# Layer 1 of a linear-attention block: sums of the last rows led ahead, denominators and scalings of two chunks placed among the other sums

## The chip, the cores and the metric

The kernel runs on one core of one Trainium2 chip. The metric is the device time in microseconds. TensorE (PE) multiplies matrices into PSUM; VectorE (DVE) and ScalarE (ACT) empty PSUM and work element by element; GpSimdE (POOL) does some of the normalisation; SyncE (SP) issues the transfers. Each engine takes its own instructions in order, and engines wait for each other with semaphores.

## The reference

Four layers run one after another on x of 2048 rows and 576 columns: linear attention (A), a two-layer perceptron with GELU (B), and A and B again with the same weights. Each is added to its input and takes a layernorm of it (B a second one). The change is in the first A alone:

```python
qkv = x @ wqkv                                # 32 heads of 18 columns
phi = lambda t: jnp.where(t > 0, t + 1, jnp.exp(t)) + 1e-6
pq, pk = phi(q), phi(k)
kv = jnp.einsum("bhsd,bhse->bhde", pk, v)
z = jnp.einsum("bhsd->bhd", pk)
num = jnp.einsum("bhqd,bhde->bhqe", pq, kv)
den = jnp.einsum("bhqd,bhd->bhq", pq, z)[..., None] + 1e-6
o = num / den                                 # then @ wo
```

## The kernel before

Rows go in 16 tiles of 128 (`NT`), queries in 4 chunks of 512 (`NCA`), and the 576 columns of heads in 5 groups: four of 7 heads (126 columns) and one of 4 (72 columns). v is never formed. The kernel sums y^T phi(k) over all rows, where y is the normalised input, and multiplies by the weights of v afterwards.

- `q_proj(g, c)` (L611) makes the queries of group g and chunk c, with five 512-column products into one PSUM bank (`q_ps`), and phi of them: two ScalarE passes (L547, L548), then VectorE's minimum and maximum (L553, L555), which writes `pq`.
- `rows_by_keys(t, half)` (L659) adds row tile t to the sums for one half (288) of the key columns. Chunks 0 to 3 are four 128-column blocks of y, in two pairs of PSUM banks; chunk 4, "the tail", is the last 64 columns of y and a column of ones, whose row of the sums is z. The sums leave PSUM behind the last tile: L681 for the tail, L684 for the others.
- `kv_groups` (L686) multiplies the sums by the weights of v and keeps the blocks of a head (`kvT`); `kv_wo_half` (L709) and `kv_wo` (L796) multiply this by wo (`kvwo`), in halves of 288 columns. The first uses single banks, the second pairs of banks.
- The z stage (L787 to L794) spreads z over the heads into `zsel`. `den_stage(c)` (L812) makes the denominators of chunk c with twenty small products and their reciprocals with ScalarE (logarithm L824, exponential L827), into the one tile `rden`. `quad_stage` (L832) spreads these on VectorE.
- `scale_stage(g, c)` (L842) spreads reciprocals over the rows of group g with one 512-column product, ScalarE copies them (L851), VectorE multiplies `pq` (L852). `quarter_stage(c)` (L856) does so for groups 0 to 3 at once: sixteen small products (32 rows of the array) into four single banks, and four ScalarE copies into the buffer `turned` (L867); `quarter_scale` (L869) multiplies (L873).
- `wo_stage(t)` (L878) makes row tile t of the output with ten 288-column products (L883), and VectorE adds the residual (L598).

PSUM has two pools: `ps_h`, four single banks with the tag "h", used in turn by `q_ps`, `k_ps`, the tail, `z_ps`, `den_ps`, `kv_ps`, `kvwo_half`, `rden_ps` and transposes; and `ps_acc`, two pairs, "accA" and "accB". A new tile waits until the last reader of the tile that had its bank is through.

The order on TensorE is the order of the program here: `pe(...)` chains its instructions. In layer 1, `q_left` holds the 20 pairs (g, c); 16 are done when the pass of the second half begins. This pass adds all 16 row tiles with their tails, with `kv_groups((0, 1))` behind tile 6 and four `kv_wo_half` behind tiles 8 to 11. After it come z, a projection, the denominators of chunk 0, `kv_groups((2, 3, 4))`, a projection, `kv_wo` and the spreads of chunk 0 in turn, a projection, the denominators of chunk 1, the last projection, and the `wo_stage` of tiles 0 to 15. Chunk 1 is spread behind tile 1 and scaled behind tile 2 (`quarter_stage(1)`, `quarter_scale`), chunks 2 and 3 later in the same way. The first tiles of the next layer's normalised rows are transposed among the last `wo_stage`s (L493), behind a chain over VectorE or ScalarE (statistics), GpSimdE (L428 to L469) and back.

Of the kernel before, what the change touches and what calls it, by code (L numbers as in the profile page):

```python
# [8 lines left out]
ALU = mybir.AluOpType  # L9
# [6 lines left out]
P = 128  # L16
NT = S // P
# [17 lines left out]
def build(tc, A_x, A_wqkv, A_wo, B_w1, B_b1, B_w2, B_b2, out, dbg=None, n_layers=4):  # L35
    nc = tc.nc
    dbg = dbg or {}
    with ExitStack() as ctx:
# [569 lines left out]
        def layer_A(li, next_kind, pre_a1=None):  # L608
            pq = {}

            def q_proj(g, c, defer=False):  # L611
                qp = ps_h.tile([P, 512], F32, name="q_ps", tag="h")
                for k in range(KD):
                    pe(nc.tensor.matmul(qp[0:GR[g], :], lhsT=wqkv_sb[:, k, GO[g]:GO[g] + GR[g]],  # L614
                                     rhs=yT[:, k, c * CA:(c + 1) * CA],
                                     start=(k == 0), stop=(k == KD - 1)))
                pq[(g, c)] = first_pq if first_pq is not None and (g, c) == (0, 0) else \
                        blk.tile([P, D], BF16, name="pq", tag="blk")
                if g == 0:
                    if first_pq is None or c > 0:  # L620
                        (nc.gpsimd if li > 0 else nc.vector).memset(pq[(g, c)][96:P, 0:CA], 1.0)
                phi = lambda after=None, dve_after=None, exp_first=False: phi_from_psum(qp[0:GR[g], :], pq[(g, c)][0:GR[g], 0:CA], GR[g], CA,
                                                       turned_cols=(li > 0), after=after, dve_after=dve_after,
                                                       exp_first=exp_first)
                if defer:
                    return phi
                phi()
# [31 lines left out]
            def rows_by_keys(t, half, chunks=(4, 0, 1, 2, 3)):  # L659
# [10 lines left out]
                if 4 not in chunks:  # L670
                    return
# [8 lines left out]
                cols = slice(half * HALF, (half + 1) * HALF)  # L680
                nc.scalar.copy(out=k2[4][0:65, cols], in_=self_k["tail"][0:65, 0:HALF])  # L681
# [27 lines left out]
            def kv_wo_half(g, half):  # L709
# [5 lines left out]
                copy = nc.vector.tensor_copy if half else nc.scalar.copy  # L715
                copy(out=kvwo[g][0:GR[g], half * HALF:(half + 1) * HALF], in_=wp[0:GR[g], 0:HALF])

            if li == 0:
                def keys(t):
                    k_half(t, 0)  # L720
                    k_half(t, 1)

                def feed_and_tick(t, n):
                    feed0(t, after=dve_last["phi"] if t > 5 else None)
                    for _ in range(n):
                        lnp.tick()

                k_half(0, 0)
                lnp.tick()
                phi = k_half(0, 1, defer=True)  # L730
                k_half(1, 0)
                feed_and_tick(3, 2)
                k_half(1, 1)
                phi()
                rows_by_keys(0, 0, (0, 1, 2, 3))
                keys(2)
                feed_and_tick(4, 2)
                rows_by_keys(1, 0, (0, 1, 2, 3))
                rows_by_keys(2, 0, (0, 1, 2, 3))
                k_half(3, 1)  # L740
                k_half(3, 0)
                q_proj(*q_left.pop(0))
                phi = q_proj(*q_left.pop(0), defer=True)
                feed_and_tick(5, 1)
                feed_and_tick(6, 2)
                phi(after=first_ones["ca4"].ins.name)
                in_order("s0a s0b g0 s1a s1b n0 nt0 g1 cd0 n1 nt1 s2a s2b g2 cd1 mi00 s3a n2 nt2 s3b ma00 g3 u3 mi10 s4a "
                         "mi11 n3 ma11 nt3 mi20 ma10 ma20 mi21 s4b ma21 g4 u4 mi01 ma01 s5a s5b mi30 g5 mi31 u5 ma30 ma31")
                in_order("ln0 re0 ln1 re1 ca0 e00 ca1 ln2 re2 id00 e01 e10 ca2 e11 id10 e20 e21 ca3 e31 e30 id30 ca4")
                rows_by_keys(3, 0, (0, 1, 2, 3))  # L750
                for t in range(4):
                    rows_by_keys(t, 0, (4,))
                for t in range(4, NT):
                    keys(t)
                    pre_a1(t)
                    if t == 4:
                        lnp.tick()
                    masks(2)
                    q_proj(*q_left.pop(0), defer=True)(after=act_last["turned"])
                    lnp.tick(transposes=0)  # L760
                    rows_by_keys(t, 0)
                for _ in range(2):
                    q_proj(*q_left.pop(0))
                masks(len(mask_steps))
            LAG = 3
            steps = [(t, 1) for t in range(NT)] if li == 0 else [(t, half) for half in range(2) for t in range(NT)]
            behind = []
            for n, (t, half) in enumerate(steps):
                if li == 0:
                    if t in (0, 1, 2):  # L770
                        wide_masks(t)
                    rows_by_keys(t, 1)
                else:
                    pre_a1(t)
                    k_half(t, half)
                    behind.append((t, half))
                    if n % 2 == 1:
                        q_proj(*q_left.pop(0))
                    if len(behind) > LAG:
                        rows_by_keys(*behind.pop(0))  # L780
                if half and t == 6:
                    kv_groups((0, 1))
                if half and t in (8, 9, 10, 11):
                    kv_wo_half((t - 8) // 2, t % 2)
            while behind:
                rows_by_keys(*behind.pop(0))
            zp = ps_h.tile([P, 512], F32, name="z_ps", tag="h")  # L787
            for g in range(G):
                pe(nc.tensor.matmul(zp[0:GR[g], g:g + 1], lhsT=k2[4][:, GO[g]:GO[g] + GR[g]], rhs=ident[:, 64:65],
                                    start=True, stop=True))  # L790
            nc.vector.tensor_tensor(out=zsel[0:126, 0:4, :], in0=head_sel[0:126, 0:4, :],
                                    in1=zp[0:126, 0:4].unsqueeze(2).to_broadcast([126, 4, H]), op=ALU.mult)
            nc.vector.tensor_tensor(out=zsel[0:72, 4, :], in0=head_sel[0:72, 4, :],
                                    in1=zp[0:72, 4:5].to_broadcast([72, H]), op=ALU.mult)  # L794

            def kv_wo(g):  # L796
                wp = ps_acc.tile([P, 2, 512], F32, name="kvwo_ps", tag=("accB", "accA")[g % 2])
                for half in range(2):
                    pe(nc.tensor.matmul(wp[0:GR[g], half, 0:HALF], lhsT=kvT[0:GR[g], g, 0:GR[g]],
                                     rhs=wo_sb[0:GR[g], g, half * HALF:(half + 1) * HALF], start=True, stop=True))  # L800
                kvwo[g] = blk.tile([P, D], BF16, name="kvwo", tag="blk")
                out = kvwo[g][0:GR[g], :].rearrange("p (h n) -> p h n", h=2)
                if g in (3, 4):
                    nc.vector.tensor_copy(out=out, in_=wp[0:GR[g], :, 0:HALF])
                else:
                    act_last["kvwo"] = nc.scalar.copy(out=out, in_=wp[0:GR[g], :, 0:HALF]).ins.name
# [70 lines left out]

            def wo_stage(t):  # L878
# [16 lines left out]
            phi = q_proj(*q_left.pop(0), defer=True)  # L895
# [273 lines left out]
```

## Time and profile before

| | us |
|---|---|
| three runs | 762.37, 762.40, 762.41 |
| the profiled execution, its own time | 762.86 |
| its span, first to last instruction | 761.1 |
| TensorE busy | 755.4 |
| ScalarE busy | 327.4 |
| VectorE busy | 271.2 |
| pass of the second half, first to last start | 58.87 to 69.63 |
| first `wo_ps` / first product of the next layer | 78.18 / 102.98 |

Times within the profile count from the start of the span. A row of the timeline gives the start, the length, the engine, the line, the operation, out<-in with partitions and elements, the number of instructions merged into it, and in brackets the idle time of that engine before it and what ended it. Matmuls overlap each other in time, so the cost of one is the distance from its start to the next start. The granted clock of TensorE is 1.00 throughout.

### The profile page before, as it was taken

How to read it: one execution, taken by the hardware profiler on the slowest of the kernel's cores; microseconds unless marked ns; L12 is line 12 of the kernel's file. 1: busy time of each engine (PE TensorE's matmuls, PEld its weight loads, DVE VectorE, ACT ScalarE, POOL GpSimd, SP SyncE). 2: the span in 40 equal slices, each digit the busy share in tenths (PEclk: the TensorE clock that was granted, in tenths of full speed). 3: DMA queues.
4: the chain of work that ended last, by engine and by line, in shares of the span. 5: the costliest groups of instructions: out<-in, count | busy, mean ns of one | idle time of the engine just before them, and what ended most of it. 6: DMA issues, size and time to landing. Idle time of an engine off the chain costs nothing.

```text
span 761.1 us, 15693 instructions
## 1 busy us (share of the span) xinstructions
PE 755.4 (99%) x6539; PEld 489.0 (64%) x6539; DVE 271.2 (36%) x683; ACT 327.4 (43%) x731; POOL 119.1 (16%) x194
## 2 busy tenths in 40 slices
PE   8999999999999999999999999999999999999998
PEld 5777654774477457646777767447645754674476
DVE  8875962136023503401455678600230132000000
ACT  6884756205600650263056566560164036205600
POOL 4840341002000301200100005300020020001000
PEclk9999999999999999999999999999999999999999
DMA  8992573017302711320246007530240033011000
GB/s 255 267 309 51 169 269 83 16 58 196 82 31 84 185 53 47 108 69 16 73 122 202 1 32 244 193 83 16 76 104 29 16 125 83 9 32 55 2 10 23
DMA packets 80897, 73.82 MB, mean 97 GB/s; under 512 B 36730, under 2 KB 65466, under 8 KB 80826
## 3 DMA queue, kind: packets, MB, share of 16 engines
q1 hardware_dynamic: 80826, 72.82, 32.9%
q8 instruction: 51, 0.84, 0.5%
q14 instruction: 20, 0.16, 0.1%
HBM read 48.03 MB, written 24.77 MB: 96 GB/s over the span
## 4 chain that ended last, share of the span: by engine, by line
PE 94%; DMA 2%; DVE 2%; ACT 1%; issue 0%; SPq 0%; DVEq 0%; ACTq 0%
PE m_ps L1060 36%; PE h_ps L1002 20%; PE hp_ps L1002 16%; PE q_ps L614 6%; PE k_ps L644 5%; PE k_ps L669 4%; PE wo_ps L883 2%; PE m_half L1060 1%; PE k_tail L669 1%; DMA xo<-x_d 1%; DMA x_d<-xo 1%; PE tp L493 1%; ACT turned L867 1%; DMA x<-in_A_x_dram 0%; PE kv_ps L693 0%
## 5 line engine op out<-in xcount | busy, mean ns | idle before, releaser
L1060 PE MATMUL m_ps<-w_sb,hT 128*128 128x288 bf16 x2232 | 274.8, 286 | 0.0
L1060 PEld LDWEIGHTS <-hT 128*128 128x128 bf16 x2304 | 224.8, 98 | 59.8 <-issue 3.4
L1002 PEld LDWEIGHTS <-w_sb 64*128 64x128 bf16 x2304 | 124.5, 94 | 136.5 <-issue 1.9
L1002 PE MATMUL hp_ps<-yT,w_sb 64*128 64x512 bf16 x1152 | 178.0, 376 | 0.0
L1002 PE MATMUL h_ps<-yT,w_sb 64*128 64x512 bf16 x1152 | 148.0, 376 | 0.0
L1007 ACT COPY relay_sb<-relay_sb 128x1 f32<-128x1 f32 x144 | 28.6, 198 | 260.2 <-PE h_ps L1002 217.9
L998 ACT ACTIVATE hT<-h_ps,b1T 128x512 bf16<-128x512 f32 x144 | 91.2, 684 | 44.4 <-PE h_ps L1002 44.4
L428 POOL TENSOR_TENSOR ln_rstd<-ln_u,neg_half 128x1 f32<-128x1 f32 x61 | 35.4, 581 | 408.3 <-DVE ln_u L410 225.3
L998 ACT ACTIVATE hT<-hp_ps,b1T 128x512 bf16<-128x512 f32 x144 | 91.2, 693 | 0.0
L598 DVE TENSOR_TENSOR xbf<-m_ps,xo 128x576 bf16<-128x576 f32 x15 | 11.4, 758 | 212.9 <-PE m_ps L1060 212.9
L598 DVE TENSOR_TENSOR xo<-m_ps,xo 128x576 f32<-128x576 f32 x16 | 12.1, 757 | 176.5 <-PE m_ps L1060 176.5
L581 POOL TENSOR_TENSOR xo<-xo,b_bc 128x576 f32<-128x576 f32 x32 | 40.9, 1284 | 101.3 <-DMA xo<-x_d 62.7
L1002 PE MATMUL h_ps<-yT,w_tail 64*128 64x512 bf16 x144 | 54.1, 376 | 0.0
L1002 PE MATMUL hp_ps<-yT,w_tail 64*128 64x512 bf16 x144 | 54.1, 376 | 0.0
L614 PE MATMUL q_ps<-yT,wqkv_sb 128*126 128x512 bf16 (+1 forms) x200 | 49.5, 379 | 0.0
L644 PE MATMUL k_ps<-wqkv_sb,yT 128*128 128x288 bf16 x320 | 47.0, 286 | 0.3 <-ACT yT L495 0.3
L883 PE MATMUL wo_ps<-kvwo,pq 126*128 126x288 bf16 (+1 forms) x320 | 44.5, 286 | 0.2
L1002 PEld LDWEIGHTS <-w_tail 64*128 64x128 bf16 x288 | 27.1, 94 | 17.1
L644 PEld LDWEIGHTS <-yT 128*128 128x128 bf16 x320 | 30.9, 98 | 8.9 <-ACT yT L495 1.0
L883 PEld LDWEIGHTS <-pq 126*128 126x128 bf16 (+1 forms) x320 | 29.8, 97 | 10.3 <-DVE pq L873 0.7
L614 PEld LDWEIGHTS <-wqkv_sb 128*126 128x126 bf16 (+1 forms) x200 | 25.4, 131 | 11.8
L295 DVE STREAM_TRANSPOSE turned<-y_ring 128x576 bf16<-128x576 bf16 x40 | 30.3, 766 | 0.4
(141 smaller groups left out, 595.7 us busy)
## 6 DMA issues: line engine op xcount, KB each, us to landing
xo<-x_d SPq DMA_DIRECT2D x48, 288.0 KB
x_d<-xo SPq DMA_DIRECT2D x32, 288.0 KB
xl<-x_d SPq DMA_DIRECT2D x24, 288.0 KB
y_d<-turned SPq DMA_DIRECT2D x40, 144.0 KB
w_sb<-in_B_w_dram SPq DMA_DIRECT2D x6, 864.0 KB
yT<-y_d SPq DMA_DIRECT2D x10, 512.0 KB
w_sb<-in_B_w_dram SPq DMA_DIRECT2D x9, 512.0 KB
x_d<-xn SPq DMA_DIRECT2D x16, 288.0 KB
```

The costliest lines, as they stand in the source:

```text
L295: turn = nc.vector.transpose(out=turned[:, :, j, :], in_=y[:, 0:D])
L428: nc.gpsimd.tensor_tensor(out=rstd[:], in0=it["u"][:], in1=neg_half[:], op=ALU.pow)
L581: nc.gpsimd.tensor_tensor(out=xo[:], in0=xo[:], in1=b2_bc[:], op=ALU.add)
L598: total = nc.vector.tensor_tensor(out=xn[:, cols].rearrange("p (h n) -> p h n", h=2), in0=halves, in1=xo[:, cols].rearrange("p (h n) -> p ...
L614: pe(nc.tensor.matmul(qp[0:GR[g], :], lhsT=wqkv_sb[:, k, GO[g]:GO[g] + GR[g]], rhs=yT[:, k, c * CA:(c + 1) * CA], start=(k == 0), stop=(k ...
L644: pe(nc.tensor.matmul(kp[:, 0:HALF], lhsT=yT[:, k, t * P:(t + 1) * P], rhs=wqkv_sb[:, k, D + half * HALF: D + (half + 1) * HALF], start=(k ...
L669: pe(nc.tensor.matmul(dst, lhsT=lhsT, rhs=pk, start=(t == 0), stop=(t == NT - 1)))
L883: pe(nc.tensor.matmul(wp[:, half, 0:HALF], lhsT=pq[(g, c)][0:GR[g], j * P:(j + 1) * P], rhs=kvwo[g][0:GR[g], half * HALF:(half + 1) * HALF ...
L998: act_last["gelu"] = nc.scalar.activation(out=to, in_=ps, func=ACT.Gelu_apprx_tanh, bias=b1T[:, f:f + 1], scale=1.0).ins.name
L1002: mm = pe(nc.tensor.matmul(dst[n], lhsT=wt, rhs=mv, start=(seen[n] == 0), stop=(seen[n] == 8)))
L1007: relay = nc.scalar.copy(out=relay_sb[:, 1:2], in_=relay_sb[:, 0:1])
L1060: pe(nc.tensor.matmul(acc[half][:, 0:HALF], lhsT=hT[f][:, j * P:(j + 1) * P], rhs=w2_sb[:, f, half * HALF:(half + 1) * HALF], start=(f == ...
```

## The change

In layer 1 alone, the pass of the second half is reordered. All sixteen tails come first, and their sums are copied out as soon as they are complete. The four-block sums follow, tile by tile, and among them are placed: z, the denominators of chunks 0 and 1, their quarter stages, the spread of group 4, all scalings of the two chunks, `kv_groups((0, 1))`, four `kv_wo_half` and two of the last four projections. Groups 0 to 3 of chunk 0 are spread by a quarter stage, where there were four `scale_stage`s. Behind the pass stay a projection, `kv_groups((2, 3, 4))`, the last projection and six `kv_wo_half` on single banks, where `kv_wo` used pairs of banks. The buffer of `pq` is now taken when phi is run and not when the products are. The second attention layer keeps its order.

```diff
@@ -614,14 +614,15 @@
...
-                pq[(g, c)] = first_pq if first_pq is not None and (g, c) == (0, 0) else \
+
+                def phi(after=None, dve_after=None):
+                    pq[(g, c)] = first_pq if first_pq is not None and (g, c) == (0, 0) else \
...
-                phi = lambda after=None, dve_after=None, exp_first=False: phi_from_psum(qp[0:GR[g], :], pq[(g, c)][0:GR[g], 0:CA], GR[g], CA,
...
+                    phi_from_psum(qp[0:GR[g], :], pq[(g, c)][0:GR[g], 0:CA], GR[g], CA, turned_cols=(li > 0), after=after,
+                                  dve_after=dve_after)
+
                 if defer:
                     return phi
                 phi()
...
-            def rows_by_keys(t, half, chunks=(4, 0, 1, 2, 3)):
+            def rows_by_keys(t, half, chunks=(4, 0, 1, 2, 3), done=True):
 
...
                     dst = self_k["tail"][0:65, 0:HALF] if k == 4 else self_k["acc"][k // 2][:, k % 2, 0:HALF]
                     lhsT = (tail_of(t) if li > 0 else first_tail(t)) if k == 4 else row_of[t][:, k * P:(k + 1) * P]
                     pe(nc.tensor.matmul(dst, lhsT=lhsT, rhs=pk, start=(t == 0), stop=(t == NT - 1)))
-                if 4 not in chunks:
+                cols = slice(half * HALF, (half + 1) * HALF)
+                if 4 in chunks and t == NT - 1:
+                    nc.scalar.copy(out=k2[4][0:65, cols], in_=self_k["tail"][0:65, 0:HALF])
+                if not done:
                     return
                 if t % 2:
                     del self_k["pk"][(half, t // 2)]
@@ -677,8 +681,6 @@
                         x0_tiles.clear()
                 if t < NT - 1:
                     return
-                cols = slice(half * HALF, (half + 1) * HALF)
-                nc.scalar.copy(out=k2[4][0:65, cols], in_=self_k["tail"][0:65, 0:HALF])
                 for i, copy in enumerate((nc.scalar.copy, nc.vector.tensor_copy)):
                     for j in range(2):
                         copy(out=k2[2 * i + j][:, cols], in_=self_k["acc"][i][:, j, 0:HALF])
...
-            def kv_wo_half(g, half):
+            def kv_wo_half(g, half, by_dve=None):
                 wp = ps_h.tile([P, 512], F32, name="kvwo_half", tag="h")
...
-                copy = nc.vector.tensor_copy if half else nc.scalar.copy
-                copy(out=kvwo[g][0:GR[g], half * HALF:(half + 1) * HALF], in_=wp[0:GR[g], 0:HALF])
...
-            LAG = 3
-            steps = [(t, 1) for t in range(NT)] if li == 0 else [(t, half) for half in range(2) for t in range(NT)]
-            behind = []
-            for n, (t, half) in enumerate(steps):
-                if li == 0:
-                    if t in (0, 1, 2):
-                        wide_masks(t)
-                    rows_by_keys(t, 1)
...
-                if half and t == 6:
-                    kv_groups((0, 1))
-                if half and t in (8, 9, 10, 11):
-                    kv_wo_half((t - 8) // 2, t % 2)
-            while behind:
-                rows_by_keys(*behind.pop(0))
-            zp = ps_h.tile([P, 512], F32, name="z_ps", tag="h")
...
+                by_dve = half if by_dve is None else by_dve
+                copy = nc.vector.tensor_copy if by_dve else nc.scalar.copy
+                copy = copy(out=kvwo[g][0:GR[g], half * HALF:(half + 1) * HALF], in_=wp[0:GR[g], 0:HALF])
+                if not by_dve:
+                    act_last["kvwo"] = copy.ins.name
+
+            def z_stage():
+                zp = ps_h.tile([P, 512], F32, name="z_ps", tag="h")
+                for g in range(G):
+                    pe(nc.tensor.matmul(zp[0:GR[g], g:g + 1], lhsT=k2[4][:, GO[g]:GO[g] + GR[g]], rhs=ident[:, 64:65],
+                                        start=True, stop=True))
...
+            if li == 0:
+
+
+                for i in range(3):
+                    wide_masks(i)
+                for t in range(NT):
+                    rows_by_keys(t, 1, (4,), done=False)
+                left = list(range(NT))
+
+                def sums(n):
+                    for _ in range(n):
+                        rows_by_keys(left.pop(0), 1, (0, 1, 2, 3))
+
+                sums(2)
+                z_stage()
+                sums(2)
+                den_stage(0)
+                quad_stage(0)
+                sums(2)
+                quarter_stage(0)
+                sums(1)
+                kv_groups((0, 1))
+                scale_stage(4, 0)
+                quarter_scale(0, (0, 1, 2, 3), after=dve_last["quad"])
+                q_proj(*q_left.pop(0))
+                sums(2)
+                den_stage(1)
+                quad_stage(1)
+                sums(2)
+                quarter_stage(1)
+                for half in range(4):
+                    kv_wo_half(half // 2, half % 2)
+                sums(1)
+                scale_stage(4, 1)
+                quarter_scale(1, (0, 1, 2, 3), after=dve_last["quad"])
+                sums(1)
+                q_proj(*q_left.pop(0))
+                sums(3)
+            else:
+                LAG = 3
...
+                z_stage()
...
-            phi = q_proj(*q_left.pop(0), defer=True)
-            den_stage(0)
-            quad_stage(0)
-            phi(after=act_last["rden"], dve_after=dve_last["quad"])
-            kv_groups((2, 3, 4))
-            late = [q_proj(*q_left.pop(0), defer=True)]
-            kv_wo(2)
-            kv_wo(3)
-            for g in range(3):
-                scale_stage(g, 0)
-            kv_wo(4)
-            scale_stage(3, 0, pair="accA")
-            late.append(q_proj(*q_left.pop(0), defer=True))
-            scale_stage(4, 0, direct=True)
-            den_stage(1, after=act_last["copy"], pair="accB")
-            quad_stage(1, after=dve_last["mult"])
-            for phi in late:
-                phi(after=act_last["rden"])
+            if li == 0:
+                q_proj(*q_left.pop(0))
+                kv_groups((2, 3, 4))
+                phi = q_proj(*q_left.pop(0), defer=True)
+                for half in range(2):
+                    for g in (2, 3, 4):
+                        kv_wo_half(g, half, by_dve=(g + half) % 2)
+                phi(after=act_last["kvwo"])
+            else:
...
-                if t == 0:
+                early = li == 0 and c == 0
+                if t == 0 and li > 0:
                     q_proj(*q_left.pop(0))
                 wo_stage(t)
                 total = dve_last["sum"]
-                if c + 1 < NCA:
+                if c + 1 < NCA and not early:
                     for g in ((), (), (0, 1, 2, 3), ())[j] if c == 0 else ((0, 1), (2, 3), (), ())[j]:
                         quarter_scale(c + 1, (g,), after=total)
                     if t == 1:
                         quarter_stage(1)
-                    if j == 3 and c + 2 < NCA:
-                        quarter_stage(c + 2)
                     if j == (2 if c == 0 else 0):
                         scale_stage(4, c + 1)
+                if j == 3 and c + 2 < NCA:
+                    quarter_stage(c + 2)
                 if j == (2 if c == 0 else 1) and c + 2 < NCA:
                     den_stage(c + 2)
                     if c > 0:
```

More of the change, by code (lines that the diff above doesn't have):

```diff
@@ L785, in layer_A @@
-            while behind:
-                rows_by_keys(*behind.pop(0))
-            zp = ps_h.tile([P, 512], F32, name="z_ps", tag="h")
[L788 to L806, printed above, removed]
+                by_dve = half if by_dve is None else by_dve
@@ new lines, in kv_wo_half @@
+                copy = nc.vector.tensor_copy if by_dve else nc.scalar.copy
[7 more added lines that the diff above has]
+                                        start=True, stop=True))
+                nc.vector.tensor_tensor(out=zsel[0:126, 0:4, :], in0=head_sel[0:126, 0:4, :],
+                                        in1=zp[0:126, 0:4].unsqueeze(2).to_broadcast([126, 4, H]), op=ALU.mult)
+                nc.vector.tensor_tensor(out=zsel[0:72, 4, :], in0=head_sel[0:72, 4, :],
+                                        in1=zp[0:72, 4:5].to_broadcast([72, H]), op=ALU.mult)
@@ new lines, in layer_A @@
+            if li == 0:
[5 more added lines that the diff above has]
+                def sums(n):
+                    for _ in range(n):
+                        rows_by_keys(left.pop(0), 1, (0, 1, 2, 3))
[22 more added lines that the diff above has]
+                sums(1)
+                q_proj(*q_left.pop(0))
+                sums(3)
+            else:
+                LAG = 3
+                behind = []
+                for n, (t, half) in enumerate((t, half) for half in range(2) for t in range(NT)):
+                    pre_a1(t)
+                    k_half(t, half)
+                    behind.append((t, half))
+                    if n % 2 == 1:
+                        q_proj(*q_left.pop(0))
+                    if len(behind) > LAG:
+                        rows_by_keys(*behind.pop(0))
+                    if half and t == 6:
+                        kv_groups((0, 1))
+                    if half and t in (8, 9, 10, 11):
+                        kv_wo_half((t - 8) // 2, t % 2)
+                while behind:
+                    rows_by_keys(*behind.pop(0))
+                z_stage()
@@ new lines, in kv_wo @@
+            def kv_wo(g):
+                wp = ps_acc.tile([P, 2, 512], F32, name="kvwo_ps", tag=("accB", "accA")[g % 2])
+                for half in range(2):
+                    pe(nc.tensor.matmul(wp[0:GR[g], half, 0:HALF], lhsT=kvT[0:GR[g], g, 0:GR[g]],
+                                     rhs=wo_sb[0:GR[g], g, half * HALF:(half + 1) * HALF], start=True, stop=True))
+                kvwo[g] = blk.tile([P, D], BF16, name="kvwo", tag="blk")
+                out = kvwo[g][0:GR[g], :].rearrange("p (h n) -> p h n", h=2)
+                if g in (3, 4):
+                    nc.vector.tensor_copy(out=out, in_=wp[0:GR[g], :, 0:HALF])
+                else:
+                    act_last["kvwo"] = nc.scalar.copy(out=out, in_=wp[0:GR[g], :, 0:HALF]).ins.name
```

120 lines of the change are left out of this document (64 added, 56 removed).

## The prediction

> **What bounds the kernel now.** I read the page's first and fourth part, then the timeline of TensorE between 57 and 103 us, which holds all that the change touches, then ScalarE's and VectorE's timelines of the same stretch.
>
> ```profile
> PE 755.4 (99%) x6539; PEld 489.0 (64%) x6539; DVE 271.2 (36%) x683; ACT 327.4 (43%) x731; POOL 119.1 (16%) x194
> PE 94%; DMA 2%; DVE 2%; ACT 1%; issue 0%; SPq 0%; DVEq 0%; ACTq 0%
> ```
>
> TensorE is busy for 755.4 of 761.1 us and is 94% of the chain that ended last. It takes its instructions in order, and nothing between the end of this stage (102.98 us, the first `h_ps`) and the end has room to take up a shift. So the change is worth what it alters in TensorE's matmul time and waits before 103 us.
>
> ```profile
> 69.75 0.47 PE L789 MATMUL z_ps<-ident,k 128*126 128x1 bf16 x5
> 70.08 1.27 PE L614 MATMUL q_ps<-yT,wqkv_sb 128*126 128x512 bf16 x5
> 71.28 0.47 PE L820 MATMUL den_ps<-pq,zsel 127*32 127x128 bf16 x20
> 74.07 0.81 PE L847 MATMUL rden_ps<-quad_rden,head_bc 128*128 128x512 bf16 x3
> 74.72 0.41 PE L799 MATMUL kvwo_ps<-wo_sb,kvT 72*72 72x288 bf16 x2
> 75.08 0.38 PE L847 MATMUL rden_pair<-quad_rden,head_bc 128*128 128x512 bf16 x1
> 75.29 1.24 PE L614 MATMUL q_ps<-yT,wqkv_sb 128*126 128x512 bf16 x5
> 78.18 2.63 PE L883 MATMUL wo_ps<-kvwo,pq 126*128 126x288 bf16 x20
> 80.74 0.45 PE L863 MATMUL rden_ps<-rden,head_bc 32*126 32x128 bf16 x16
> 81.12 1.40 PE L883 MATMUL wo_ps<-kvwo,pq 126*128 126x288 bf16 x10
> 82.36 0.38 PE L847 MATMUL rden_ps<-quad_rden,head_bc 128*128 128x512 bf16 x1
> 84.79 1.89 PE L883 MATMUL wo_ps<-kvwo,pq 126*128 126x288 bf16 x10
> 86.76 0.39 PE L847 MATMUL rden_ps<-quad_rden,head_bc 128*128 128x512 bf16 x1
> ```
>
> Matmuls are pipelined, so their cost is the distance between starts. Ten `wo_ps` take 81.12 to 82.36 = 1.24 us in the clear, but the ten from 84.79 take 1.97 us to the next start: a wait of 0.73 us. The weight loads say for what:
>
> ```profile
> 85.09 0.10 PEld L883 LDWEIGHTS <-pq 126*128 126x128 bf16 x1 [0.20 <-DVE pq L873]
> 85.42 0.10 PEld L883 LDWEIGHTS <-pq 126*128 126x128 bf16 x1 [0.24 <-DVE pq L873]
> 85.76 0.60 PEld L883 LDWEIGHTS <-pq 72*128 72x128 bf16 x6 [0.24 <-DVE pq L852]
> ```
>
> Row tile 4, the first of chunk 1, waits for VectorE's scaling of that chunk. Everything else there stands close: the seam that the change attacks, sums to denominators (69.75 to 71.28), already has a query projection over it.
>
> **The change, part by part.** Prices are distances between starts: 0.1225 us for a 288-column product, 0.216 for a 512-column one.
>
> *Removed waits.* The 0.73 us goes, since chunk 1 is scaled before the pass ends. The `rden_pair` wait goes too: two products from 74.72 need 0.245 and the next starts after 0.36, 0.115 us. So do some 0.15 us at `z_ps` (0.33 us for five one-column products, some 0.10 of it waiting for the copy) and in the `kv_ps` behind the denominators. Together 1.0 us.
>
> *Removed matmul time.* Four wide spreads of chunk 0 (74.07 to 74.72 and 75.08 to 75.29, 0.86 us) become one quarter stage: 80.74 to 81.12 = 0.38 us, plus 0.10 us going into small tiles (20 `wo_ps` to 80.74 took 2.56 us for 2.45). Saved 0.38 us. [...]
>
> *Moved at no cost.* The sixteen tail products, the sums, the four query projections, two denominators and kv groups keep count and size; four tails one after another already run at 0.122 us from 17.34 us on. The six kv·wo products of groups 2 to 4 stay six. SyncE's and GpSimdE's queues keep their order; the residual loads wait for sums that finish at most some 7 us later, long before their rows are used. The three mask expansions still stand on VectorE ahead of `zsel` (to 62.42 us).
>
> *Added waits.* A quarter stage takes all four single PSUM banks (the pool `ps_h`), and ScalarE alone empties them.
>
> ```profile
> 65.28 0.40 ACT L716 CAST kvwo<-kvwo_half 126x288 bf16<-126x288 f32 x1 [5.07 <-PE kvwo_half L711]
> 71.85 0.26 ACT L824 ACTIVATE den_ps<-den_ps 128x128 f32<-128x128 f32 x1 [1.40 <-issue]
> 72.14 0.28 ACT L827 ACTIVATE rden<-den_ps 128x128 bf16<-128x128 f32 x1
> 81.22 2.05 ACT L867 CAST turned<-rden_ps 126x512 bf16<-126x512 f32 x4 [0.50 <-PE rden_ps L863]
> ```
>
> The copies start 0.48 us after the stage's first matmul and last 2.05 us: 0.61 for one, 0.48 apart. With 0.05 us from an engine's end to TensorE's start (a VectorE copy ends at 75.03, `rden_pair` starts at 75.08) the banks are free 1.14, 1.62, 2.10 and 2.58 us after the first matmul, while TensorE is through after 0.38. Today `wo_ps` products follow, which use the other two pairs of banks, and the next `ps_h` tile comes 1.62 us after the start (82.36). In the changed kernel `ps_h` tiles follow at once. I lay TensorE out from the first sum of the second half, 58.87 us in both kernels:
>
> - 16 tails, 8 sums, z (0.25), 8 sums, denominators 0 (0.50 with its change of tile), 8 sums, change: quarter stage 0 starts at 64.62, is done at 65.00; 4 sums to 65.49. `kv_ps` waits for bank one until 65.76: **0.27**. Its ten products, one spread, then the query projection waits for bank three (66.72) from 66.55: **0.17**.
> - Projection (1.08), 8 sums, denominators 1, 8 sums: quarter stage 1 starts at 70.36, done at 70.74. Now four kv·wo halves come with nothing before them. The first waits until 71.50, **0.76**; the second 0.36, the third 0.36; the fourth takes the bank that VectorE frees from the second (0.33 to the copy, 0.46 for it, 0.05): 0.24. Together **1.72**. Behind them in TensorE's queue stand the last eight sums and all else.
> - Sums, spread, two projections (4.83 us), kv groups 2 to 4 (0.75), projection: six kv·wo halves at 79.60. They share four banks; the fourth waits for ScalarE's copy of the first (0.32 + 0.40 + 0.05): 0.40, the fifth 0.06. Together **0.46**.
> - Row tile 2 waits for the bank pair of tile 0: ScalarE's two passes over the last projection now stand behind three copies, VectorE's sum of tile 0 behind that projection's maximum; it ends at 83.36 where the products would begin at 83.24, so with 0.05 and the weight load **0.21**.
>
> Added 2.83 us. [...]
>
> *Bounds.* The trace shows no `ps_h` tile directly behind a quarter stage. From below the new waits cost nothing, as behind 80.74 us; from above, as if TensorE stood through all of both copy runs, 2 x (2.58 - 0.38) + 0.67 = 5.1 us. I take 2.83, nearest to the copy rows themselves, as the positions of the tiles behind it are fixed.
>
> *Sum.* 2.83 - 1.0 - 0.38 = +1.45 us; laid out on to row tile 5 the same path starts it at 88.35 instead of 86.99 us, +1.36. I take +1.4. The profiled execution took 762.86 us around its span of 761.1, 0.46 above the median of 762.40 that the runs show; put on the median: 763.8 us.
>
> **The rivals.**
> - *The banks are there in time (not slower).* Place: behind the two quarter stages. If the tiles found free banks, 2.16 us of waits go: 0.67 - 1.38 = -0.7, 761.7 us. It turns where less than 0.7 of the 2.16 is left. For it: after 80.74, 84.41 and 91.56 no product waits for a copy. Against it: there the followers use other banks. 0.08, of which 0.03 for a gain above 0.2%.
> - *The denominators come late.* From first denominator product to usable reciprocals: 71.28 to 72.42, 1.19 with the hop; quarter stages 0 and 1 then have 0.29 us to spare, `zsel` behind the masks about as much. Half a microsecond late at each of the three: +0.6, 764.4 us. For it: VectorE and ScalarE get these among other work. Against it: both idle there today (ScalarE 5.07 us before 65.28). 0.17.
> - *The normalisation of the next layer comes late.* The third row tile's last block is normalised at 97.43, its last transpose runs at 97.61, 0.18 to spare; GpSimdE took 1.63 us for one such tile and 0.82 for another. One more slow pass: 0.81 - 0.18 = +0.6, 764.4 us. Against it: the order behind the denominators of chunk 3 is unchanged on all engines. 0.08.
> - *The clock falls.* If the granted clock, 1.00 through this profile, halved for the 4.83 us behind the cluster of 1.72 us, +4.8: 768.6 us. No row shows it, not even 0 to 5 us, where TensorE is busy 3.60. 0.03. [...]
>
> **How the numbers follow.** The forecast, waits of about the size laid out, has 0.58, from 763.4 to 764.3 us; smaller ones (762.8 to 763.4) 0.06. The range 762.8 to 764.8 leaves out the first rival, the clock and the far ends of the two late ones, under 2 in 10. About 0.2% (1.52 us: 760.88 and 763.92) is what a measurement of this kernel can tell from no change. Above 763.92 lie some four tenths of the forecast (0.24), nearly all of the two late ones (0.24) and the clock (0.03): slower 0.51. Faster 0.03, the rest 0.46.
>
> **What would show it.** Right: `kv_ps` of groups 0 and 1 and the first four `kvwo_half` stand behind ScalarE's copies out of `rden_ps`, some 1.7 us of waits in the latter; row tile 4 follows tile 3 with no wait; `h_ps` starts near 104.4. Wrong: `kvwo_half` close behind the quarter stage, a wait of row tile 4 that is still there, or a quarter stage that waits for `rden`.

## The result, and the profile after

| | median, us | lowest to highest | ratio to before (95%) |
|---|---|---|---|
| kernel before, 17 runs | 762.45 | 762.32 to 763.70 | |
| changed kernel, 17 runs | 763.83 | 763.68 to 764.46 | 1.0017 (1.0010 to 1.0025) |

The changed kernel is 1.4 us slower, and the interval of the ratio does not hold 1. Its profiled execution took 763.80 us, with a span of 762.1 us and a granted clock of 1.00. The first product of the next layer (`h_ps`) starts at 104.33 us, the pass of the second half at 58.82. That is 45.51 us, against 44.11 before, 1.40 more: the whole loss lies in the stage that was changed. (The spans differ by 1.0 only, since the profiled execution of before was above its median and lost 0.35 us behind this stage.)

The first two parts of the page of the changed kernel that bear on it (busy time of the engines; shares of the chain that ended last):

```profile
PE 755.5 (99%) x6551; PEld 489.2 (64%) x6551; DVE 271.3 (36%) x684; ACT 328.7 (43%) x734; POOL 117.7 (15%) x194
...
PE 97%; DVE 1%; ACT 1%; DMA 0%; issue 0%
```

TensorE's busy time is that of before within 0.1 us. The row of one product lasts 0.28 us where the next could start 0.1225 us after it, so a part of each wait counts as busy, and the starts tell more. This is the timeline of TensorE in the changed kernel, where L788 is the quarter stage, L713 the kv·wo halves, L772 the wide spread, L695 the kv groups, L614 the projection, L670 the sums and L924 the output:

```profile
64.55 0.45 PE L788 MATMUL rden_ps<-rden,head_bc 32*126 32x128 bf16 x16
64.93 0.66 PE L670 MATMUL k_ps<-pk,x 128*128 128x288 bf16 x4
65.66 0.73 PE L695 MATMUL kv_ps<-k,wqkv_sb 128*126 128x126 bf16 x10
66.23 0.38 PE L772 MATMUL rden_ps<-quad_rden,head_bc 128*128 128x512 bf16 x1
66.64 1.24 PE L614 MATMUL q_ps<-yT,wqkv_sb 128*126 128x512 bf16 x5
...
70.27 0.45 PE L788 MATMUL rden_ps<-rden,head_bc 32*126 32x128 bf16 x16
71.38 0.28 PE L713 MATMUL kvwo_half<-wo_sb,kvT 126*126 126x288 bf16 x1 [0.66 <-ACT turned L792]
71.87 0.28 PE L713 MATMUL kvwo_half<-wo_sb,kvT 126*126 126x288 bf16 x1 [0.21 <-ACT turned L792]
72.36 0.62 PE L713 MATMUL kvwo_half<-wo_sb,kvT 126*126 126x288 bf16 x2 [0.21 <-ACT turned L792]
72.82 0.66 PE L670 MATMUL k_ps<-pk,x 128*128 128x288 bf16 x4
...
79.47 0.53 PE L713 MATMUL kvwo_half<-wo_sb,kvT 126*126 126x288 bf16 x3
80.24 0.59 PE L713 MATMUL kvwo_half<-wo_sb,kvT 126*126 126x288 bf16 x3 [0.24 <-ACT kvwo L719]
...
86.73 1.40 PE L924 MATMUL wo_ps<-kvwo,pq 126*128 126x288 bf16 x10
88.11 0.39 PE L772 MATMUL rden_ps<-quad_rden,head_bc 128*128 128x512 bf16 x1
```

Three things are visible. After the sixteen products of each quarter stage TensorE stands before a tile of `ps_h`: the four halves of kv·wo, which need 0.1225 us each, start at 71.38, 71.87, 72.36 and 72.70 us. At 79.47 three of six halves pass and the fourth waits for the copy of the first. And the ten products of row tile 4, from 86.73 us, now take 1.38 us to the next start, where they took 1.97. The timelines of ScalarE and VectorE show what the halves wait for:

```profile
65.02 2.05 ACT L792 CAST turned<-rden_ps 126x512 bf16<-126x512 f32 x4 [0.81 <-PE rden_ps L788]
...
70.74 2.05 ACT L792 CAST turned<-rden_ps 126x512 bf16<-126x512 f32 x4 [0.82 <-PE rden_ps L788]
...
72.19 0.46 DVE L719 CAST kvwo<-kvwo_half 126x288 bf16<-126x288 f32 x1 [1.80 <-PE kvwo_half L713]
```

Four copies of 2.05 us together stand behind 0.38 us of products. The first three halves start as ScalarE's copies end, some 0.49 us apart. The fourth does not wait for ScalarE's last copy, which ends at 72.79 us: it takes the bank of the second half, which VectorE's copy frees at 72.65, and starts at 72.70.

### The profile page after: what moved, and what is told of

Read it like the earlier page. It is cut to its first block, busy times and chain, and to the rows that moved or that the text cites. A ratio compares the mean times of both kernels' runs of the same rounds, so it can differ in the third digit from the quotient of the medians.

```text
span 762.1 us, 15720 instructions
## 1 busy us (share of the span) xinstructions
PE 755.5 (99%) x6551; PEld 489.2 (64%) x6551; DVE 271.3 (36%) x684; ACT 328.7 (43%) x734; POOL 117.7 (15%) x194
## 4 chain that ended last, share of the span: by engine, by line
PE 97%; DVE 1%; ACT 1%; DMA 0%; issue 0%
PE m_ps L1111 36%; PE h_ps L1053 20%; PE hp_ps L1053 16%; PE q_ps L614 6%; PE wo_ps L924 5%; PE k_ps L645 5%; PE k_ps L670 4%; PE m_half L1111 1%; PE k_tail L670 1%; PE tp L493 1%; PE kv_ps L695 0%; PE den_ps L745 0%; PE rden_ps L772 0%; PE rden_ps L788 0%; DMA x<-in_A_x_dram 0%; PE kvwo_half L713 0%
## 5 line engine op out<-in xcount | busy, mean ns | idle before, releaser
L614 PE MATMUL q_ps<-yT,wqkv_sb 128*126 128x512 bf16 (+1 forms) x200 | 49.4, 379 | 0.0
L924 PE MATMUL wo_ps<-kvwo,pq 126*128 126x288 bf16 (+1 forms) x320 | 43.7, 286 | 0.0
L924 PEld LDWEIGHTS <-pq 126*128 126x128 bf16 (+1 forms) x320 | 30.0, 97 | 9.3 <-DVE pq L798 0.2
L614 PEld LDWEIGHTS <-wqkv_sb 128*126 128x126 bf16 (+1 forms) x200 | 25.6, 131 | 11.9 <-issue 0.3
L547 ACT ACTIVATE phi_e<-q_ps 126x512 bf16<-126x512 f32 (+1 forms) x40 | 23.9, 598 | 15.4 <-PE q_ps L614 15.4
```

Of the source, the lines that this page charges most:

```text
L547: exp = nc.scalar.activation(out=e_out, in_=ps_ap, func=ACT.Exp)
L924: pe(nc.tensor.matmul(wp[:, half, 0:HALF], lhsT=pq[(g, c)][0:GR[g], j * P:(j + 1) * P], rhs=kvwo[g][0:GR[g], half * HALF:(half + 1) * HALF ...
```

## The experiments

All eight kernels were run beside the kernel before: the first four on one chip (before: median 762.65 us in 33 runs), the last four on another (762.48 in 27 runs). In the expectations A is the theory of the prediction, that the loss is TensorE waiting for banks which ScalarE alone empties; B is the rival of each run. Distances "from the pass to `h_ps`" are from the first sum of the second half to the first `h_ps`, in the profiled execution of each kernel: 44.11 us before, 45.51 in the changed kernel.

### late_halves: something between the quarter stage and the halves

```diff
                 quarter_stage(1)
-                for half in range(4):
-                    kv_wo_half(half // 2, half % 2)
+                sums(2)
+                kv_wo_half(0, 0)
+                sums(1)
+                kv_wo_half(0, 1)
+                kv_wo_half(1, 0)
                 sums(1)
                 scale_stage(4, 1)
                 quarter_scale(1, (0, 1, 2, 3), after=dve_last["quad"])
+                kv_wo_half(1, 1)
+                phi = q_proj(*q_left.pop(0), defer=True)
                 sums(1)
-                q_proj(*q_left.pop(0))
-                sums(3)
+                phi()
```

> Behind quarter stage 1 two row tiles of sums come first, then the four kv-wo halves one or two at a time with sums between them; the phi passes of the last projection of the pass run behind the copies of the sums. Nothing else is moved. Theory A (the loss is TensorE waiting for single PSUM banks that ScalarE empties): of the 1.69 us of waits in the four halves some 0.1 to 0.2 stay, so 763.8 - 1.6 = 762.2 us (762.0 to 762.6), about equal to the kernel before. Theory B (the loss sits in what the change adds to TensorE's own time, tile changes and the second set of small products, or it comes back in the row tiles behind): the waits move to the next place, 763.5 to 763.9 us.

Measured: 762.53 us (762.32 to 763.00, 11 runs), 0.9997 of before (0.9988 to 1.0005). From the pass to `h_ps` it takes 43.97 us, 1.54 less than in the changed kernel. TensorE's timeline of this kernel at the same place:

```profile
70.40 0.45 PE L788 MATMUL rden_ps<-rden,head_bc 32*126 32x128 bf16 x16
70.78 1.15 PE L670 MATMUL k_ps<-pk,x 128*128 128x288 bf16 x8
71.77 0.29 PE L713 MATMUL kvwo_half<-wo_sb,kvT 126*126 126x288 bf16 x1
...
72.39 0.41 PE L713 MATMUL kvwo_half<-wo_sb,kvT 126*126 126x288 bf16 x2
...
73.34 0.29 PE L713 MATMUL kvwo_half<-wo_sb,kvT 126*126 126x288 bf16 x1
```

The same instructions run, and none of the halves waits: each stands where its bank is free. Only the projection behind the last of them waits, for 0.12 us. The copies are no shorter (2.06 us in den2_between, which has the same order here); they run beside sums that use the other two pairs of banks. So the four halves right behind the quarter stage cost the whole 1.4 us, as A has it, and what the change takes away elsewhere just pays for the rest.

### cover_quarter0: one more tile of sums behind the first quarter stage

```diff
                 quarter_stage(0)
-                sums(1)
+                sums(2)
                 kv_groups((0, 1))
...
                 q_proj(*q_left.pop(0))
-                sums(2)
+                sums(1)
                 den_stage(1)
```

> One row tile of sums is moved from behind the first projection of the pass to behind quarter stage 0, where two now stand. Theory A: the waits of kv_ps (0.23) and of the projection (0.19) go, 763.4 us. Theory B: no change, 763.8 us. If the reciprocals of chunk 1 are then late for quarter stage 1 nothing shows here, since its sums still number two.

Measured: 763.69 us (763.41 to 764.55, 11 runs), 1.0011 of before (1.0002 to 1.0019). The median lies between the two theories and settles nothing. The trace does: neither `kv_ps` nor the projection waits any longer, and from the pass to `h_ps` it takes 45.09 us, 0.42 less. The lowest runs differ by 0.27 us from those of the changed kernel. Together with late_halves the same move was then worth 0.41 us of median (below, though across two chips), which is the size of the two waits, 0.23 and 0.19.

### split_copies: VectorE makes two of the four copies

```diff
                 for i in range(4):
+                    if li == 0 and c < 2 and i % 2:
+                        nc.vector.tensor_copy(out=spread_rows[0:126, i, 0:4 * P], in_=banks[i][0:126, :])
+                        continue
                     act_last["copy"] = nc.scalar.copy(out=spread_rows[0:126, i, 0:4 * P], in_=banks[i][0:126, :]).ins.name
```

> In quarter stages 0 and 1 VectorE copies two of the four banks, ScalarE the other two. The banks are free about 1.1, 1.2, 1.6 and 1.8 us after the first product where they were 1.1, 1.6, 2.1 and 2.6. Theory A: the first wait stays (0.73), the later ones shrink from 0.96 to some 0.5 and the projection's 0.19 goes: 763.1 us (762.9 to 763.4). Theory B: no change, 763.8 us.

Measured: 763.38 us (763.07 to 764.05, 11 runs), 1.0006 of before (0.9997 to 1.0015), 0.45 less than the changed kernel by the medians, 0.72 less from the pass to `h_ps` (44.79 us). TensorE's timeline of this kernel:

```profile
70.28 0.45 PE L788 MATMUL rden_ps<-rden,head_bc 32*126 32x128 bf16 x16
71.39 1.07 PE L713 MATMUL kvwo_half<-wo_sb,kvT 126*126 126x288 bf16 x4 [0.66 <-ACT turned L795]
72.31 0.65 PE L670 MATMUL k_ps<-pk,x 128*128 128x288 bf16 x4
```

The first half still waits 0.73 us, the length of one copy and the way to it, but the second follows at once. The four together now take 0.92 us instead of 1.44, and the projection's wait behind quarter stage 0 is gone. Here a second engine shortens the run of copies and leaves the first wait at 0.73 us, and so gives less (0.72 us) than covering the copies does (1.54 in late_halves).

### wide_chunk0: chunk 0 by four wide spreads, as before

```diff
-                quarter_stage(0)
+                for g in range(4):
+                    scale_stage(g, 0)
                 sums(1)
                 kv_groups((0, 1))
                 scale_stage(4, 0)
-                quarter_scale(0, (0, 1, 2, 3), after=dve_last["quad"])
```

> Chunk 0 is spread by four scale stages again, in the place of quarter stage 0; all else as in the changed kernel. Theory A: TensorE's 0.38 us come back and the waits behind quarter stage 0 (0.43) go, but the spreads wait for VectorE's spread of the reciprocals (some 0.3): 764.1 us (763.8 to 764.3). Theory B (the extra set of small products and its two changes of tile cost more than the wide spreads): 763.3 us or less.

Measured: 764.17 us (764.03 to 765.36, 11 runs), 1.0020 of before (1.0011 to 1.0029); 0.34 slower than the changed kernel by the medians, 0.23 from the pass to `h_ps` (45.74 us). TensorE's timeline of this kernel:

```profile
64.77 1.02 PE L772 MATMUL rden_ps<-quad_rden,head_bc 128*128 128x512 bf16 x3
65.63 0.65 PE L670 MATMUL k_ps<-pk,x 128*128 128x288 bf16 x4
66.12 0.74 PE L695 MATMUL kv_ps<-k,wqkv_sb 128*126 128x126 bf16 x10
```

Four spreads take 0.86 us, 64.77 to 65.63 (the row counts three; the record of one is missing, and its 0.216 us are there). Behind them `kv_ps` and the projection wait for nothing. Before them TensorE stands for 0.27 us, and VectorE's timeline of this kernel has the reason:

```profile
64.29 0.43 DVE L759 TENSOR_TENSOR quad_rden<-quad_mask,rden 128x512 bf16<-128x512 bf16 x1 [1.57 <-ACT rden L752]
```

The wide form needs VectorE's spread of the reciprocals, which ends at 64.72. So 0.86 + 0.27 = 1.13 us stands against 0.48 + 0.23 + 0.19 = 0.90 for the quarter stage with its waits: 0.23, as in the trace. The saving of 0.38 us is there, but at this place it comes to 0.23, since the waits behind the quarter stage are the longer ones by 0.15.

### late_and_covered: both moves together

The edits of late_halves and cover_quarter0 in one kernel.

> The two reorderings together: two row tiles of sums behind quarter stage 0, and the four kv-wo halves late behind quarter stage 1. Theory A: their gains add up, since each takes away its own waits: 762.5 - 0.45 = 762.0 us (761.7 to 762.3), some 0.5 us under the kernel before. Theory B (what one gains is paid back in the next wait, at the six halves or the row tiles): 762.5 us.

Measured: 762.12 us (761.87 to 763.12, 11 runs), 0.9993 of before (0.9984 to 1.0002), and 43.55 us from the pass to `h_ps`. The gains add, as A has it: 1.54 and 0.42 are 1.96, and the two kernels differ by 45.51 - 43.55 = 1.96 us. By the medians this kernel and the one before can't be told apart. TensorE still waits 0.47 us among the six halves (0.405 before the fourth), 0.16 at row tile 2, 0.146 behind row tile 4 and 0.125 at a projection.

### den2_between: work between the six halves as well

On top of late_and_covered the denominators of chunk 2 move from behind row tile 2 to between the third and fourth of the six halves, into a pair of banks that is free there.

```diff
                     for g in (2, 3, 4):
                         kv_wo_half(g, half, by_dve=(g + half) % 2)
+                    if half == 0:
+                        den_stage(2, pair="accB")
...
-                    den_stage(c + 2)
+                    if not early:
+                        den_stage(c + 2)
```

> On top of the two reorderings the denominators of chunk 2 are made between the two groups of three of the six kv-wo halves behind the pass, in a pair of banks, where they stood behind row tile 2. Theory A: 0.47 us of waits of the fourth and fifth half and the 0.16 of row tile 2 go, 761.3 us (761.0 to 761.7), 0.15% under the kernel before. Theory B (the wait for ScalarE only moves, now behind two more passes): 762.0 us.

Measured: **761.16 us** (761.01 to 761.34, 11 runs), 0.9981 of before (0.9972 to 0.9990). This kernel beats both. TensorE's timeline of it:

```profile
77.59 0.53 PE L713 MATMUL kvwo_half<-wo_sb,kvT 126*126 126x288 bf16 x3
78.05 0.47 PE L745 MATMUL den_pair<-pq,zsel 127*32 127x128 bf16 x20
78.45 0.58 PE L713 MATMUL kvwo_half<-wo_sb,kvT 126*126 126x288 bf16 x3
78.87 5.10 PE L928 MATMUL wo_ps<-kvwo,pq 126*128 126x288 bf16 x40
```

Three waits go with one move: the fourth half's 0.405, that of row tile 2 (forty `wo_ps` now run without a break), and that behind row tile 4, before the spread of chunk 2's reciprocals. They add up to 0.71 us, and the distance to `h_ps` falls by 0.73 (42.82 us). The medians differ by 0.96, the profiled executions by 0.70 (761.89 and 761.19 us): the rest is the spread of the runs of late_and_covered, six of which lie 0.25 us or more above its lowest.

The first two waits went as planned, the third by luck. Theory A had not counted it, and it did not go because the reciprocals were earlier. VectorE's spread of them (`quad_rden`) starts 0.86 us after the first product of quarter stage 2 in this kernel (84.75 after 83.89) and in late_and_covered (85.30 after 84.44). But here it takes 0.42 us, and there 0.85:

```profile
84.75 0.42 DVE L759 TENSOR_TENSOR quad_rden<-quad_mask,rden 128x512 bf16<-128x512 bf16 x1
```

### copies_twice: the suspected cost doubled

```diff
                 for i in range(4):
                     act_last["copy"] = nc.scalar.copy(out=spread_rows[0:126, i, 0:4 * P], in_=banks[i][0:126, :]).ins.name
+                    if li == 0 and c == 1:
+                        act_last["copy"] = nc.scalar.copy(out=spread_rows[0:126, i, 0:4 * P], in_=banks[i][0:126, :]).ins.name
```

Each copy of the second quarter stage is made twice, the changed kernel being otherwise as it is.

> The changed kernel with each of the four ScalarE copies of quarter stage 1 made twice. Nothing else. It doubles the suspected cost: the banks are free 1.6, 2.6, 3.5 and 4.5 us after the first product. Theory A: the four halves wait 1.5 us longer in all, 765.3 us (765.0 to 765.6). Theory B (ScalarE is not on the path): 763.8 us.

Measured: 767.13 us (767.08 to 767.83, 5 runs), 1.0059 of before (1.0046 to 1.0071), 3.30 us above the changed kernel, where A expected 1.5 and B none. TensorE's timeline of this kernel:

```profile
72.70 0.28 PE L713 MATMUL kvwo_half<-wo_sb,kvT 126*126 126x288 bf16 x1 [1.64 <-ACT turned L794]
73.19 0.28 PE L713 MATMUL kvwo_half<-wo_sb,kvT 126*126 126x288 bf16 x1 [0.21 <-ACT turned L794]
74.02 0.28 PE L713 MATMUL kvwo_half<-wo_sb,kvT 126*126 126x288 bf16 x1 [0.55 <-DVE kvwo L719]
74.66 0.28 PE L713 MATMUL kvwo_half<-wo_sb,kvT 126*126 126x288 bf16 x1 [0.36 <-ACT turned L794]
...
76.60 2.30 PE L614 MATMUL q_ps<-yT,wqkv_sb 128*126 128x512 bf16 x5
...
80.21 1.24 PE L614 MATMUL q_ps<-yT,wqkv_sb 128*126 128x512 bf16 x5
```

The halves wait 1.70, 0.37, 0.71 and 0.52 us, 3.30 instead of 1.69: 1.6 us more, close to the 1.5 that A expected. The rest is another cost, and the two rows of the projection show it: the same five products take 2.30 us at 76.60 and 1.24 at 80.21. The table of TensorE by windows in this kernel (window, its length, PE busy and instructions, granted clock, DMA share, GB/s) says why:

```profile
66.00:71.00 5.00, 4.96 (x68) 1.00 0.02 4
71.00:75.20 4.20, 1.45 (x14) 1.00 0.00 0
75.20:78.70 3.50, 3.50 (x12) 0.52 0.02 5
78.70:82.00 3.30, 3.30 (x33) 0.99 0.00 0
```

Behind the cluster of waits the granted clock is 0.52 for some 3.5 us. Products of 288 columns then start 0.240 us apart instead of 0.1225, those of 512 columns 0.427 instead of 0.216; from 75.28 to 78.74 us that comes to about 1.7 us. All five runs of this kernel have a mean clock of 0.998, so the fall is not that of one execution. So A's price of the waits holds, and the rival named in the prediction as the clock is real, though not in the changed kernel. The same view of the changed kernel:

```profile
66.00:70.50 4.50, 4.47 (x65) 1.00 0.02 4
70.50:73.00 2.50, 1.37 (x22) 1.00 0.00 0
73.00:78.00 5.00, 5.00 (x38) 1.00 0.02 3
```

### tails_first: the tails alone

In the kernel before, all sixteen tails lead the pass and their sums are copied at once; nothing else is moved.

```diff
...
                 if li == 0:
-                    if t in (0, 1, 2):
-                        wide_masks(t)
-                    rows_by_keys(t, 1)
+                    if t == 0:
+                        for i in range(3):
+                            wide_masks(i)
+                        for row in range(NT):
+                            rows_by_keys(row, 1, (4,), done=False)
+                    rows_by_keys(t, 1, (0, 1, 2, 3))
```

> The kernel before with only one part of the change: the sixteen tails lead the pass of the second half and their sums are copied at once. The number of products and their order behind the pass stay. Theory A: no cost, and the 0.1 us at z_ps goes: 762.3 us (762.2 to 762.5). Theory B (sixteen 65-column loads in a row hold TensorE): 0.2 us or more above the kernel before.

Measured: 762.38 us (762.31 to 763.13, 11 runs), 0.9994 of before (0.9985 to 1.0002), and 44.02 us from the pass to `h_ps`, 0.09 less than before. Leading with the tails costs nothing and gives next to nothing by itself: z no longer waits for the copy, which was priced at about 0.10 us (its five products take 0.24 us to the next start, 0.33 in the kernel before).

## Why the prediction was right, point by point

The forecast of 763.8 us was met (763.83), and the terms behind it can be set against the trace of the changed kernel.

| term | forecast, us | trace |
|---|---|---|
| `kv_ps` behind quarter stage 0 | +0.27 | +0.23 |
| projection behind it | +0.17 | +0.19 |
| four kv·wo halves behind quarter stage 1 | +1.72 | +1.69 |
| six kv·wo halves | +0.46 | +0.47 |
| row tile 2 | +0.21 | +0.16 |
| wait in and behind row tile 4 | -0.73 | -0.58 |
| other removed waits | -0.27 | -0.34 |
| matmul time of the wide spreads | -0.38 | -0.39 |
| stage, laid out / measured | +1.36 | +1.40 |

- **The new waits** are right in place, releaser and size: 2.74 us against 2.83. For the four halves the waits are 0.73, 0.37, 0.37 and 0.22 us; the first row's distance holds 0.10 more for the change out of small tiles, which is not a wait (behind quarter stage 0, where nothing waits, the next product starts 0.149 us after the last small one; from the third group of four small ones to the fourth it is 0.047). That they set the end, and are not only seen, is shown by late_halves (take away 1.69, gain 1.5) and copies_twice (double the copies, lose 1.6 in waits). Taking ScalarE's durations from the rows behind 80.74 us of the kernel before held: 2.05 us for four there and here.
- **The bounds** of 0 and 5.1 us for them were wide, and the choice of 2.83 by laying out bank after bank was what made the forecast. With the copies shared by ScalarE and VectorE (split_copies) the kernel takes 0.72 us less from the pass to `h_ps`; moving the halves behind some sums, late_halves, gave 1.54.
- **The removed wait of row tile 4** was too large a term, since its rows were misread in part. The prediction puts all of the 0.73 us down to scaled rows of chunk 1 that come late. By the starts of the ten products these waits are 0.05, 0.21 and 0.21, together 0.48 us, and they are gone. The other 0.25 stood behind the ten products, before the spread of chunk 2's reciprocals, as a weight load of the kernel before shows:

```profile
86.76 0.10 PEld L847 LDWEIGHTS <-head_bc 128*128 128x128 bf16 x1 [0.40 <-DVE quad_rden L834]
```

  Of this wait 0.146 us stay. The timelines of VectorE and GpSimdE in the changed kernel have

```profile
86.53 0.76 DVE L598 TENSOR_TENSOR xn<-wo_ps,xo_pair 128x576 f32<-128x576 f32 x1 [0.67 <-POOL ln_rstd L428]
87.20 0.85 DVE L759 TENSOR_TENSOR quad_rden<-quad_mask,rden 128x512 bf16<-128x512 bf16 x1
...
86.96 0.82 POOL L461 TENSOR_SCALAR y_ring<-xn,ln_rstd,ln_nmr 128x576 bf16<-128x576 f32 x1
```

  VectorE's spread ends at 88.05, 0.06 us ahead of TensorE's. In 0.43 us, as at 64.25, it would have ended at 87.63, before TensorE came to it (87.97). So the prediction took the spread behind row tile 4 as ready, in both kernels, and followed only the path to row tile 5.
- **The saved matmul time** is as forecast; wide_chunk0 shows that the wide form would at this place have a wait of its own (0.27 us for VectorE's spread), so that a part of what the quarter stage's waits cost here is given back.
- **Moved at no cost** held for the tails: tails_first runs as fast as before.
- **The rivals.** Banks in time: excluded, of the 2.16 us forecast behind the two quarter stages 2.11 are there. Late denominators: the reciprocals are there at 64.22 and 69.93 us, the quarter stages start at 64.55 and 70.27, so the slack of about 0.3 held. Late normalisation: no transpose at the end of the stage waits (the `wo_ps` ahead of the last three take 0.123 to 0.124 us each). The clock stays at 1.00 in this stage; in copies_twice, with 3.30 us of waits in the cluster instead of 1.69, it fell to 0.52 for one stretch of 3.5 us, which cost 1.7 us of time, not the 4.8 that the rival was given. One ground for the small chance of this rival, that no row shows a halved clock, was misread: the first products of the kernel before start 0.427 us apart, later ones of the same shape 0.216 (last section).

The small removed waits can be told apart in the rows of the two kernels: 0.09 us at `z_ps`, 0.11 at `rden_pair`, 0.05 at the `kv_ps` behind the denominators, and 0.09 that the prediction had not seen. This last is at the first product of three projections (70.08, 72.47 and 77.08 us in the kernel before), which took 0.245 us to the next start, where the others took 0.216. With them the terms of the trace add up to 1.43 us, and the stage measures 1.40. The forecast's terms were off by 0.15 at row tile 4, by 0.09 in the new waits and by 0.07 in the small removed ones, and these errors cancel in part: that the mechanism was right is shown, that the forecast was met within 0.03 us is partly luck.

## What to carry to other kernels

Where a short TensorE stage fills every bank of a pool, look at what follows it: here the last copy ended 2.52 us after the first of 0.38 us of products (70.27 to 72.79), the four halves behind them waited 1.69 us for banks of that pool, and with sums first, which use other banks, the same instructions took 1.54 us less from the pass to `h_ps`. Such waits can be forecast from the rows of a kernel that does not have them yet: lay out bank by bank who frees it and when, and follow the operands of the next product too, not only the path that was late before. Once a gap is known, a good filler is work that makes another place wait, as the denominators of chunk 2 did: one move ended two waits as planned, and a third by chance.

## What the runs showed of the hardware

In one kernel the clock fell behind a cluster of waits. With TensorE busy 1.37 of 2.50 us (changed kernel, from 70.50) the granted clock stayed at 1.00; with 1.45 of 4.20 us (copies_twice, from 71.00) it was 0.52 for about 3.5 us, beginning half a microsecond after TensorE was at work again (75.28 after 74.78), and waits of 1.6 us more cost 3.3. No run lies between the two, and what sets the start and the length of the slow stretch is not shown.

The clock was not at 1.00 throughout, as the part ahead of the prediction has it. The profile's clock column has 1.00 from the start, but the rows of the kernel before have

```profile
1.31 3.60 PE L214 MATMUL warm_ps<-y_ring 128*128 128x512 bf16 x9 [1.31 <-DVE y_ring L209]
```

Up to 4.27 us these products start 0.427 us apart, as in the slow stretch of copies_twice, and at 5.62 the same product takes 0.216. The changed kernel begins in the same way (also 0.427 us apart up to 4.27 us), and it bears on no comparison of the stage.

Also new was that one VectorE instruction of one shape (`quad_rden`, 128x512) took 0.43 us at 64.25 and 0.85 us at 87.20 in the same profile. The ten profiles have it 80 times. It took 0.85 or 0.86 us in the seven cases where GpSimdE's normalisation (L461) ran beside it, as in the rows at 86.96 and 87.20 above, and 0.41 to 0.43 us in the other 73. That the one slows the other is argued from this; no run moved one of them alone.
